# A two-layer decode kernel: the attention's matrix steps in column tiles of 32, and work moved between the engines

## The chip, the cores and the metric

The kernel runs on one core of a Trainium2 chip. The core has TensorE (PE in the profile; its weight loads are PEld), VectorE (DVE), ScalarE (ACT), GpSimd (POOL), and SyncE (SP), which here issues the transfers. 16 DMA engines carry data from the device's memory (HBM) into the on-chip memory of 128 partitions. TensorE writes into accumulator banks of 128 x 512 fp32 words. The metric is the device time of one execution in microseconds. The kernel before took 1196.09 us in the median of three runs (1195.54 to 1197.15).

## The reference, cut to what matters

One token for each of 8 batch elements goes twice through attention and a dense block; both rounds use the same caches and weights:

```python
x = x + A(layernorm(x));  x = x + B(layernorm(x))     # and the same two lines again
def A(x):                       # B=8, D=512, 32 query heads on 8 kv heads, 8192 keys of 128
    q = x @ wq                  # [8, 32, 128]
    p = softmax(q . k_cache / sqrt(128))
    return (p @ v_cache) @ wo   # caches [8, 8, 8192, 128] bf16
def B(x): return silu(x @ w1) @ w2          # 512 -> 1792 -> 512
```

Each cache holds 134 MB, far more than on-chip memory, and both are needed in both rounds.

## The kernel before, in words

*Tasks and positions.* A task is one round, batch element and kv head: 2 x 8 x 8 = 128 tasks. A task has 8 positions of 1,024 keys; two positions are a granule, the unit of a load: 2,048 keys x 128 channels of bf16, 0.524 MB. `make_tasks` mixes both rounds. For 5 of 8 kv heads (20 granules) K stays on chip between the rounds, so that it is loaded once: 352 loads of K in all, and 512 of V.

*Loads.* An arena of 27 slots (`NSLOT`) takes the granules. `plan_loads` sorts all loads by the position that needs them and gives each the slot that is free first. SP issues them in that order (`issue_until`, lines 411 to 413), each when the last reader of its slot is done. `issue` (L357) builds the source. For K, partition p receives 16 neighbouring keys, 4 KB, with a step of 64 keys (16 KB) from one partition to the next; a V granule is contiguous, 4 KB for each partition:

```python
src = cache[d.b, d.g].rearrange("(p k c) d -> k p (c d)", k=NGRAN, p=128)[d.k]   # K, L360
src = cache[d.b, d.g].rearrange("(k p c) d -> k p (c d)", k=NGRAN, p=128)[d.k]   # V, L362
```

*The steps of a task.* `emit_t` (L440): one VectorE transpose of 32x32 blocks per K granule, in place. `emit_q`: four matmuls spread the query over the rows and a VectorE multiply (L466) makes QB. `emit_s` (L473): scores, 32 matmuls per granule; four of them write to partition groups 0, 32, 64 and 96 of a bank, the form that the profile calls 128*32. Then the softmax: `softmax_max` takes the row maxima (L491) and spreads them (L493), `softmax_shift` brings them to all rows by a matmul with ones (L501) and takes the minimum of each row (L504, L507), `softmax_exp` (L511) exponentiates on ScalarE and sums each row, `softmax_sum` gathers the sums of a head (L518) and adds them over the partitions on GpSimd (L521), `emit_pt` transposes P with four matmuls (L530) and copies it to PT (L534), and `softmax_rcp` takes reciprocals (L541). `emit_pv` (L543): 64 matmuls per task with a V chunk as the stationary operand and 4 columns of PT, each repeated 12 times (`PVN`), as the moving one: 128 x 48 into OTp. `emit_norm` (L561) multiplies by the reciprocals.

*Between the attentions.* `wo_part` adds each head's product with wo in the bank MISC; `block_stages` holds residual, LayerNorm (`ln_stages`), both dense projections (`project`) and silu. For all but the last batch element of a round these are single-token pieces of a list `chain`, a few of which are put between the positions; at the very end the last round runs for all 8 tokens at once (the tail).

*Order.* One loop over positions p (L770) writes every engine's program. At odd p it emits the scores of positions p - 1 and p, and PV for positions that lie `LP` = 14 back; the softmax steps of the task before come at the phases in `soft`; the transposes run `LT` = 2 positions ahead. Each engine works strictly in the order written, and waits on semaphores that `Sync` derives from named resources.

Of the kernel before, what the change touches and what calls it, by code (L numbers as in the profile page):

```python
# [5 lines left out]
HQ = 32  # L6
DH = 128
# [5 lines left out]
GRP = 8  # L13
# [6 lines left out]
LP = 14  # L20
EARLY = 4
WO_FROM = 36
NTP = 2
# [7 lines left out]
PVN = 12  # L31
# [177 lines left out]
def _build(ctx, nc, A_x, A_k_cache, A_v_cache, A_wq, A_wo, B_w1, B_w2, out):  # L209
# [63 lines left out]
    own_q = sb([128, NQ], FP32, "own_q")  # L273
    pick = sb([128, NPART, 128], BF16, "pick")
# [5 lines left out]
    s1 = sb([128, B], FP32, "s1")  # L280
    s1a = sb([128, B], FP32, "s1a")
# [3 lines left out]
    eh = sb([128, FT * B], FP32, "eh")  # L285
# [5 lines left out]
    ones = sb([128, 128], FP32, "ones")  # L291
# [9 lines left out]
    ssa = [sb([128, REP], FP32, "ssa") for _ in range(NST)]  # L301
# [6 lines left out]
    QSp = ps_bank("QSp")  # L308

# [47 lines left out]
    def issue(d):  # L357
        cache = A_k_cache if d.kind == "K" else A_v_cache
        if d.kind == "K":
            src = cache[d.b, d.g].rearrange("(p k c) d -> k p (c d)", k=NGRAN, p=128)[d.k]  # L360
        else:
            src = cache[d.b, d.g].rearrange("(k p c) d -> k p (c d)", k=NGRAN, p=128)[d.k]  # L362
        dst = ARENA[:, d.slot * SLOT:(d.slot + 1) * SLOT]
        dma(sp, dst, src, slsem[d.slot], writes=[r_half(d.slot, 0), r_half(d.slot, 1)])
        (k_slot if d.kind == "K" else v_slot)[(d.b, d.g, d.k)] = d.slot

    with nc.Block() as block:

        @block.sync
        def _(sync_eng):  # L370
# [11 lines left out]
            op(dve, lambda: dve.memset(ones[:, :], 1.0), writes=["ones"])  # L382
            for n in range(NQB):
                op(pool, lambda n=n: pool.memset(QB[n][:, :, :], 0.0), writes=[f"QB{n}"])
# [9 lines left out]
                own_q[:, :], ident[:, :].rearrange("p (c q) -> p c q", q=QUAD), AX.X, ALU.add),  # L394
               reads=["ident"], writes=["own_q"])
            for i in range(NPART):
                op(dve, lambda i=i: dve.tensor_copy(
                    pick[:, i, :].rearrange("p (a r) -> p a r", a=NQ),
                    ident[:, i // 2 * 2 * QUAD:(i // 2 + 1) * 2 * QUAD].rearrange("p (r e) -> p e r", e=2)[:, i % 2]
                    .unsqueeze(1).to_broadcast([128, NQ, QUAD])),  # L400
                   reads=["ident"], writes=["pick"])
            for c in range(NQ):
# [4 lines left out]
                   reads=["hm", "real"], writes=["far"])  # L407

# [44 lines left out]
            def emit_q(ti):  # L453
# [7 lines left out]
                for i in range(NPART):  # L461
                    at = (n * NPART + i) * REP
                    steps.append(lambda i=i, at=at: pe.matmul(  # L463
                        QSp[:, at:at + REP], pick[:, i, :], q, start=True, stop=True))
                mm_group(steps, reads=["pick", rq], writes=[f"QS{n}"])
                op(dve, lambda: dve.tensor_tensor(  # L466
                    QB[n][:, :, 0:USED].rearrange("p i (r a) -> p i r a", a=NQ),
                    QSp[:, n * NPART * REP:(n + 1) * NPART * REP].rearrange("p (i r) -> p i r", r=REP).unsqueeze(3)
                    .to_broadcast([128, NPART, REP, NQ]),
                    own_q[:, :].unsqueeze(1).unsqueeze(1).to_broadcast([128, NPART, REP, NQ]), ALU.mult),  # L470
                   reads=[f"QS{n}", "own_q"], writes=[f"QB{n}"])
# [17 lines left out]
            def softmax_max(ti):  # L489
# [3 lines left out]
                op(dve, lambda: dve.tensor_scalar(  # L493
                    spread[:, :].rearrange("p (c q) -> p c q", q=USED), lanes, rowmax[:, 0:1], -SM_SCALE,
                    op0=ALU.mult, op1=ALU.mult),
                   reads=["ident", "rowmax"], writes=["spread"])

            def softmax_shift(ti):
                ob = ti % 2
                every = OTp[ob][:, 0:NQ * USED]  # L500
                mm_group([lambda: pe.matmul(every, ones[:, :], spread[:, :], start=True, stop=True)],  # L501
# [7 lines left out]
            def softmax_exp(ti):  # L509
                bank, st = ti % NSCP, ti % NST  # L510
                op(act, lambda: act.activation(  # L511
                    P[:, :].rearrange("p (x j k) -> p k x j", x=CPB, k=NGRAN),
                    SCp[bank][:, :].rearrange("p (k x j) -> p k x j", k=NGRAN, x=CPB), ACT.Exp, bias=shift[:, 0:1], scale=SM_SCALE, accum_out=rs[st][:, :]),
                   reads=[f"SC{bank}", "shift"], writes=["P", f"rs{st}"])

            def softmax_sum(ti):
                st = ti % NST
                op(dve, lambda: dve.tensor_scalar(  # L518
                    ssm[st][:, :], hm[:, :], rs[st][:, 0:1], None, op0=ALU.mult),
                   reads=["hm", f"rs{st}"], writes=[f"ssm{st}"])  # L520
                op(pool, lambda: pool.partition_all_reduce(ssa[st][:, :], ssm[st][:, :], 128, bass.bass_isa.ReduceOp.add),  # L521
                   reads=[f"ssm{st}"], writes=[f"ssa{st}"])

            def emit_pt(ti):
# [5 lines left out]
                    lambda c=c: pe.transpose(tpv[:, c, :], P[:, c * 128:(c + 1) * 128], ident[:, :])  # L530
                    for c in range(CPB)
                ]
                mm_group(steps, reads=["P", "ident"], writes=[f"TP{tb}"])
                op(dve, lambda: dve.tensor_copy(  # L534
# [4 lines left out]
            def softmax_rcp(ti):  # L539
                st = ti % NST  # L540
                op(dve, lambda: dve.reciprocal(rcp[st][:, :], ssa[st][:, :]), reads=[f"ssa{st}"], writes=[f"rcp{st}"])  # L541

            def emit_pv(i):  # L543
# [5 lines left out]
                otp = OTp[ob][:, 0:REP * PVN].rearrange("p (r n) -> p r n", n=PVN)  # L549
                steps = []  # L550
                for c in range(GRP):
                    cc = (i % GPT) * GRP + c
                    steps.append(
                        lambda c=c, cc=cc: pe.matmul(  # L554
                            otp, chunk(slot, h * GRP + c), pv[:, cc % CPB, cc // CPB % NQ, k, :].unsqueeze(2).to_broadcast([128, REP, PVN]),
                            start=(cc == 0), stop=(cc == NCH - 1),
                        )
                    )
                mm_group(steps, reads=[r_half(slot, h), f"PT{pb}"], writes=[f"OT{ob}"])

            def emit_norm(ti):  # L561
# [6 lines left out]
                op(dve, lambda: dve.tensor_tensor(dst, OTp[ob][:, 0:REP * PVN:PVN], rcp[st][:, :], ALU.mult),  # L568
                   reads=[f"OT{ob}", f"rcp{st}"], writes=[rd])

            def ln_stages(xv, rx, n):

                xcv, sqv, xnv = xc[:, :, 0:n], sq[:, :, 0:n], xnT[:, :, 0:n]

                def first():
                    op(dve, lambda: dve.tensor_reduce(s1[:, 0:n], xv.rearrange("p k b -> p b k"), AX.X, ALU.add),
                       reads=[rx], writes=["s1"])
                    op(pool, lambda: pool.partition_all_reduce(s1a[:, 0:n], s1[:, 0:n], 128, bass.bass_isa.ReduceOp.add),
                       reads=["s1"], writes=["s1a"])

                def second():
                    op(
                        dve,
                        lambda: dve.scalar_tensor_tensor(
                            xcv, s1a[:, 0:n].unsqueeze(1).to_broadcast([128, KT, n]), -1.0 / D, xv,
                            op0=ALU.mult, op1=ALU.add,
                        ),
                        reads=["s1a", rx], writes=["xc"],
                    )
                    op(dve, lambda: dve.tensor_tensor(sqv, xcv, xcv, ALU.mult), reads=["xc"], writes=["sq"])  # L590
                    op(dve, lambda: dve.tensor_reduce(s1[:, 0:n], sqv.rearrange("p k b -> p b k"), AX.X, ALU.add),
                       reads=["sq"], writes=["s1"])
                    op(pool, lambda: pool.partition_all_reduce(s1a[:, 0:n], s1[:, 0:n], 128, bass.bass_isa.ReduceOp.add),
# [265 lines left out]
```

## Time and profile before

| What | Value |
|---|---|
| median of three runs | 1196.09 us |
| the profiled execution's own time | 1198.79 us |
| its span, first to last instruction | 1197.1 us |
| busy: PE, PEld | 839.0 us (70%), 673.4 us (56%) |
| busy: DVE, ACT, POOL | 736.1 (61%), 183.5 (15%), 70.8 us (6%) |
| bytes moved by DMA | 468.06 MB, mean 391 GB/s |
| mean granted TensorE clock | 0.663 |

In the page's rows by slices each digit is the busy share of one fortieth of the span in tenths. In a group of instructions the line number, engine and operation come first, then output and inputs by the program's names, shapes and count, then busy time, mean duration in ns, and the engine's idle time before the group with what ended it. "Time to landing" of a load runs from its issue to the arrival of its last byte. Rows by stretches give start and end, length, busy time of PE, PEld, DVE, ACT and POOL with instruction counts, the granted clock, the mean busy share of the 16 DMA engines and the rate in GB/s.

### The profile page before, as it was taken

To read this page: it belongs to the slowest core of one execution; us is meant where nothing else is said; L and a number is where in the kernel's file an instruction comes from. 1 tells how busy PE (TensorE), PEld (TensorE's weight loads), DVE (VectorE), ACT (ScalarE), POOL (GpSimd) and SP (SyncE) were. 2 spreads that over 40 slices of the span, in tenths; PEclk is the share of its full clock that TensorE was granted. 3 is DMA by queue.
4 is the path that set the end of the run, shared out by engine and by line. 5 is a ranking of instruction groups with operands and counts; after the bars stand their busy time and mean duration, and the time that the engine had idled before them with its cause. 6 is when DMAs were issued, how large, how long until landed. Compare 5 with 4: busy or idle time off the path is not lost.

```text
span 1197.1 us, 46189 instructions
## 1 busy us (share of the span) xinstructions
PE 839.0 (70%) x20984; PEld 673.4 (56%) x20984; DVE 736.1 (61%) x1830; ACT 183.5 (15%) x266; POOL 70.8 (6%) x172
## 2 busy tenths in 40 slices
PE   1636677767776677767777778777776777677785
PEld 1435566556655566556665566556665656555564
DVE  3736763767456673867457763867376755768464
ACT  0101112111111012111111111111111111111111
POOL 0000000000000000000000000000000000000000
PEclk9955568555765577655866586756775587657765
DMA  9999999999999999999999999999999999999994
GB/s 368 385 396 397 399 355 408 407 394 395 393 408 407 368 389 401 408 404 395 389 408 408 388 397 409 407 402 395 393 407 403 399 393 408 407 392 386 402 408 165
DMA packets 131619, 468.06 MB, mean 391 GB/s; under 512 B 13904, under 2 KB 19808, under 8 KB 130912
## 3 DMA queue, kind: packets, MB, share of 16 engines
q1 hardware_dynamic: 131424, 465.12, 99.1%
q8 instruction: 164, 2.69, 0.9%
q14 instruction: 31, 0.25, 0.1%
HBM read 465.05 MB, written 0.01 MB: 388 GB/s over the span
## 4 chain that ended last, share of the span: by engine, by line
DMA 40%; PE 31%; DVE 15%; issue 9%; SPq 3%; ACT 2%; POOL 0%; POOLq 0%; ACTq 0%; DVEq 0%
DMA arena<-in_A_v_cache_dram 37%; PE OTp L554 14%; PE SCp L481 8%; DVE arena L444 7%; SPq L339 3%; DMA arena<-in_A_k_cache_dram 3%; PE MISC L634 3%; PE OTp L501 2%; PE TPp L530 2%; ACT P L511 2%; DVE rowmax L491 1%; DVE PT L534 1%; PE MISC L652 1%; DVE tr L607 1%; DVE spread L493 1%
## 5 line engine op out<-in xcount | busy, mean ns | idle before, releaser
L554 PE MATMUL OTp<-PT,arena 128*128 128x48 bf16 x8192 | 381.1, 205 | 227.6 <-DMA arena<-in_A_v_cache_dram 182.1
L444 DVE STREAM_TRANSPOSE arena<-arena 128x1024 int32<-128x1024 int32 x352 | 434.9, 1236 | 115.9 <-DMA arena<-in_A_k_cache_dram 115.2
L554 PEld LDWEIGHTS OTp<-PT,arena 128*128 128x128 bf16 x8192 | 316.9, 110 | 331.5 <-DMA arena<-in_A_v_cache_dram 242.6
L511 ACT ACTIVATE P<-SCp,shift 128x512 bf16<-128x512 f32 x128 | 180.3, 1409 | 930.6 <-DVE shift L507 651.5
L481 PE MATMUL SCp<-arena,QB 128*32 128x128 bf16 x8192 | 287.0, 275 | 37.3 <-issue 29.0
L481 PEld LDWEIGHTS SCp<-arena,QB 128*32 128x32 bf16 x8192 | 161.4, 115 | 84.1 <-issue 48.6
L521 POOL PARTITION_ALL_REDUCE ssa<-ssm x128 | 55.6, 435 | 996.0 <-DVE ssm L518 970.8
L534 DVE COPY PT<-TPp 128x256 bf16<-128x256 bf16 x128 | 37.3, 291 | 103.6 <-PE TPp L530 101.8
L501 PE MATMUL OTp<-spread,ones 128*128 128x64 f32 x256 | 75.4, 389 | 25.9 <-DVE spread L493 22.7
L491 DVE TENSOR_REDUCE rowmax<-SCp 128x1 f32<-128x512 f32 x128 | 84.8, 663 | 11.5 <-PE SCp L481 10.3
L530 PE MATMUL TPp<-ident,P 128*128 128x128 bf16 x512 | 68.8, 278 | 13.7 <-ACT P L511 9.6
L504 DVE SCALAR_TENSOR_TENSOR own<-OTp,real,far 128x64 f32<-128x64 f32 x128 | 32.9, 257 | 71.7 <-PE OTp L501 71.7
L501 PEld LDWEIGHTS OTp<-spread,ones 128*128 128x128 f32 x256 | 54.9, 266 | 35.6 <-DVE spread L493 34.4
L518 DVE TENSOR_SCALAR ssm<-hm,rs 128x4 f32<-128x4 f32 x128 | 26.8, 210 | 73.9 <-ACT P L511 73.9
L530 PEld LDWEIGHTS TPp<-ident,P 128*128 128x128 bf16 x512 | 41.7, 122 | 16.5 <-ACT P L511 12.3
L634 PE MATMUL MISC<-xnT,wq 128*128 128x32 bf16 (+1 forms) x1152 | 37.1, 185 | 19.3 <-DVE xnT L621 13.1
L634 PEld LDWEIGHTS MISC<-xnT,wq 128*128 128x128 bf16 x1152 | 35.8, 105 | 20.4 <-issue 16.3
L652 PE MATMUL MISC<-at,wo 128*128 128x32 bf16 x1024 | 37.7, 185 | 6.1 <-issue 4.4
L652 PEld LDWEIGHTS MISC<-at,wo 128*128 128x128 bf16 x1024 | 33.2, 103 | 6.9 <-issue 4.6
L463 PE MATMUL QSp<-QT,pick 128*128 128x4 bf16 x512 | 32.5, 168 | 5.7 <-DVE QT L717 2.9
L493 DVE TENSOR_SCALAR spread<-ident,rowmax 128x64 f32<-128x64 bf16 x128 | 32.6, 255 | 4.5
L511 ACT ACTIVATION_READ_ACCUMULATOR P<-SCp,shift 128x1 f32 x128 | 33.3, 260 | 0.0
(54 smaller groups left out, 276.3 us busy)
## 6 DMA issues: line engine op xcount, KB each, us to landing
arena<-in_A_v_cache_dram SPq DMA_DIRECT2D x512, 512.0 KB, 10.3
arena<-in_A_k_cache_dram SPq DMA_DIRECT2D x352, 512.0 KB, 14.5
wq<-in_A_wq_dram SPq DMA_DIRECT2D x1, 4096.0 KB, 16.6
wo<-in_A_wo_dram SPq DMA_DIRECT2D x1, 4096.0 KB, 26.3
w<-in_B_w_dram SPq DMA_DIRECT2D x2, 1792.0 KB, 22.8
P<-in_A_x_dram SPq DMA_DIRECT2D x1, 8.0 KB
out_dram<-P SPq DMA_DIRECT2D x1, 8.0 KB
```

The lines of the kernel that those rows point to most:

```text
L444: op(dve, lambda: dve.transpose(words, words), reads=[r_half(slot, 0), r_half(slot, 1)], writes=[r_half(slot, 0), r_half(slot, 1)])
L481: lambda n=n, t=t: pe.matmul(SCp[bank][t * QUAD:(t + 1) * QUAD, k * 128:(k + 1) * 128], QB[qn][:, n, :], keys[:, t, n // 2, n % 2], start= ...
L491: op(dve, lambda: dve.tensor_reduce(rowmax[:, :], SCp[bank][:, :], AX.X, ALU.max), reads=[f"SC{bank}"], writes=["rowmax"])
L493: op(dve, lambda: dve.tensor_scalar(spread[:, :].rearrange("p (c q) -> p c q", q=USED), lanes, rowmax[:, 0:1], -SM_SCALE, op0=ALU.mult, op ...
L501: mm_group([lambda: pe.matmul(every, ones[:, :], spread[:, :], start=True, stop=True)], reads=["ones", "spread"], writes=[f"OT{ob}"])
L511: op(act, lambda: act.activation(P[:, :].rearrange("p (x j k) -> p k x j", x=CPB, k=NGRAN), SCp[bank][:, :].rearrange("p (k x j) -> p k x ...
L521: op(pool, lambda: pool.partition_all_reduce(ssa[st][:, :], ssm[st][:, :], 128, bass.bass_isa.ReduceOp.add), reads=[f"ssm{st}"], writes=[f ...
L530: lambda c=c: pe.transpose(tpv[:, c, :], P[:, c * 128:(c + 1) * 128], ident[:, :])
L534: op(dve, lambda: dve.tensor_copy(PT[pb][:, :, :].rearrange("p x (c q) -> p x c q", q=USED), tpv.rearrange("p x (c q) -> p x c q", q=QUAD) ...
L554: lambda c=c, cc=cc: pe.matmul(otp, chunk(slot, h * GRP + c), pv[:, cc % CPB, cc // CPB % NQ, k, :].unsqueeze(2).to_broadcast([128, REP, P ...
L634: lambda o=o, k=k: pe.matmul(MISC[:, o * n:o * n + w], w_sb[:, k, o * 128:(o + 1) * 128], rhs_of(k).to_broadcast([128, w]) if n == 1 else ...
L652: lambda o=o, h=h: pe.matmul(MISC[:, o * w:(o + 1) * w], wo_sb[:, h, o * 128:(o + 1) * 128], rhs_of(h).to_broadcast([128, w]) if n == 1 el ...
```

## The change

The keys of a K granule are dealt to the partitions differently: partition 32a + j takes 16 keys from block a (2,048 keys) of the head, so the source is 4 blocks of 32 neighbouring pieces of 4 KB. A granule's P can then be transposed in pieces of 32 columns, and `softmax_exp` writes P without reordering. All attention matmuls write to groups of 32 partitions: query spreading (16 matmuls per task), the spreading of the maxima (4), transposes (16), and PV, which now has 4 columns of PT as the stationary operand and a V chunk of 128 columns as the moving one, in four partition groups whose partial sums `emit_fold` adds. Sums over partitions (softmax and LayerNorm) become matmuls with ones, residuals matmuls with the identity. ScalarE takes the copies out of the accumulator banks and the two scalings (spread, ssm); GpSimd takes the Newton steps of the single-token LayerNorm and the products of silu, which is computed from tanh instead of exp. `LP` goes from 14 to 12, and the phases of the softmax steps change (`SOFT`). The diff, cut to its core:

```diff
-LP = 14
+LP = 12
+SOFT = (0, 1, 2, 3, 4, 4, 6)
-NTP = 2
+NTP = 1
-PVN = 12
...
         if d.kind == "K":
-            src = cache[d.b, d.g].rearrange("(p k c) d -> k p (c d)", k=NGRAN, p=128)[d.k]
+            src = cache[d.b, d.g].rearrange("(a k j c) d -> k a j (c d)", a=NQ, k=NGRAN, j=QUAD)[d.k]
...
-                    steps.append(lambda i=i, at=at: pe.matmul(
-                        QSp[:, at:at + REP], pick[:, i, :], q, start=True, stop=True))
...
+                    for a in range(NQ):
+                        steps.append(lambda a=a, at=at, pairs=pairs: pe.matmul(
+                            QSp[a * QUAD:(a + 1) * QUAD, at + a:at + USED:NQ], pairs, q, start=True, stop=True))
+                mm_group(steps, reads=["ident", rq], writes=["QS"])
+                op(act, lambda: act.copy(
+                    QB[n][:, :, 0:USED],
...
-                op(dve, lambda: dve.tensor_scalar(
-                    spread[:, :].rearrange("p (c q) -> p c q", q=USED), lanes, rowmax[:, 0:1], -SM_SCALE,
+                op(act, lambda: act.activation(
+                    spread[:, :].rearrange("p (c q) -> p c q", q=USED), lanes, ACT.Copy, scale=rowmax[:, 0:1]),
...
-                mm_group([lambda: pe.matmul(every, ones[:, :], spread[:, :], start=True, stop=True)],
+                mm_group([lambda t=t: pe.matmul(every[t * QUAD:(t + 1) * QUAD, :], ones[:, :], spread[:, :], start=True, stop=True)
+                          for t in range(NQ)],
...
-                    P[:, :].rearrange("p (x j k) -> p k x j", x=CPB, k=NGRAN),
-                    SCp[bank][:, :].rearrange("p (k x j) -> p k x j", k=NGRAN, x=CPB), ACT.Exp, bias=shift[:, 0:1], scale=SM_SCALE, accum_out=rs[st][:, :]),
+                    P[:, :], SCp[bank][:, :], ACT.Exp, bias=shift[:, 0:1], scale=SM_SCALE, accum_out=rs[st][:, :]),
...
+                op(act, lambda: act.activation(ssm[st][:, :], hm[:, :], ACT.Copy, scale=rs[st][:, 0:1]),
...
-                op(pool, lambda: pool.partition_all_reduce(ssa[st][:, :], ssm[st][:, :], 128, bass.bass_isa.ReduceOp.add),
-                   reads=[f"ssm{st}"], writes=[f"ssa{st}"])
+            def softmax_all(ti):
+                st = ti % NST
+                mm_group([lambda t=t: pe.matmul(sums[t * QUAD:(t + 1) * QUAD, :], ones[:, :], ssm[st][:, :],
+                                                start=True, stop=True) for t in range(NQ)],
...
+                        tpv[k * QUAD:(k + 1) * QUAD, c, :], P[:, k * 128 + c * QUAD:k * 128 + (c + 1) * QUAD], ident[:, :])
+                    for c in range(CPB) for k in range(NGRAN)
...
-                op(dve, lambda: dve.tensor_copy(
+                op(act, lambda: act.copy(
                     PT[pb][:, :, :].rearrange("p x (c q) -> p x c q", q=USED),
...
-                            otp, chunk(slot, h * GRP + c), pv[:, cc % CPB, cc // CPB % NQ, k, :].unsqueeze(2).to_broadcast([128, REP, PVN]),
-                            start=(cc == 0), stop=(cc == NCH - 1),
+                            OTp[ob][t * QUAD:t * QUAD + REP, 0:DH], pv[:, cc % CPB, cc // CPB % NQ, k, :], chunk(slot, h * GRP + c),
+                            start=(cc < NQ), stop=(cc >= NCH - NQ),
...
+            def emit_fold(ti):
+                ob = ti % 2
+                op(act, lambda: act.copy(OS[:, :], OTp[ob][:, 0:DH]), reads=[f"OT{ob}"], writes=["OS"])
+                folded = OTp[ob][:, DH + NQ * USED:DH + NQ * USED + REP]
+                mm_group([lambda t=t: pe.matmul(folded[t * QUAD:(t + 1) * QUAD, :], OS[:, t * QUAD:(t + 1) * QUAD], pick[:, :],
...
+                    mm_group(steps, reads=[rx, "ident", "mean"], writes=["MISC"])
+                    op(act, lambda: act.activation(sqv, mid, ACT.Square), reads=["MISC"], writes=["sq"])
+                    op(act, lambda: act.copy(xcv, mid), reads=["MISC"], writes=["xc"])
...
-                            op(dve, lambda: dve.tensor_scalar(t, y, y, v, op0=ALU.mult, op1=ALU.mult),
+                            op(pool, lambda: pool.tensor_scalar(t, y, y, v, op0=ALU.mult, op1=ALU.mult),
...
+                    op(act, lambda: act.activation(th[:, 0:FT * n], MISC[:, 0:FT * n], ACT.Tanh, scale=0.5),
+                       reads=["MISC"], writes=["th"])
...
+                    op(pool, lambda: pool.tensor_scalar(th[:, 0:FT * n], th[:, 0:FT * n], 1.0, None, op0=ALU.add),
+                       reads=["th"], writes=["th"])
+                    op(pool, lambda: pool.tensor_tensor(hsT[:, 0:FT * n], th[:, 0:FT * n], hx[:, 0:FT * n], ALU.mult),
+                       reads=["th", "hx"], writes=["hsT"])
...
-            soft = {0: [softmax_max], 2: [softmax_shift, softmax_exp], 4: [softmax_sum], 5: [emit_pt], 7: [softmax_rcp]}
+            stages = (softmax_max, softmax_shift, softmax_exp, softmax_sum, emit_pt, softmax_all, softmax_rcp)
+            soft = {ph: [f for f, at in zip(stages, SOFT) if at == ph] for ph in SOFT}
...
+                    emit_fold(tj)
                     emit_norm(tj)
```

## The prediction

> **What bounds the kernel now.** I read the header and the slices first, then the DMA queues, then the chain that ended last, and then the DMA share and the landing times stage by stage. The page:
>
> ```profile
> span 1197.1 us, 46189 instructions
> PE   1636677767776677767777778777776777677785
> DMA  9999999999999999999999999999999999999994
> GB/s 368 385 396 397 399 355 408 407 394 395 393 408 407 368 389 401 408 404 395 389 408 408 388 397 409 407 402 395 393 407 403 399 393 408 407 392 386 402 408 165
> q1 hardware_dynamic: 131424, 465.12, 99.1%
> DMA 40%; PE 31%; DVE 15%; issue 9%; SPq 3%; ACT 2%; POOL 0%; POOLq 0%; ACTq 0%; DVEq 0%
> DMA arena<-in_A_v_cache_dram 37%; PE OTp L554 14%; PE SCp L481 8%; DVE arena L444 7%; SPq L339 3%; DMA arena<-in_A_k_cache_dram 3%; PE MISC L634 3%; PE OTp L501 2%; PE TPp L530 2%; ACT P L511 2%; DVE rowmax L491 1%; DVE PT L534 1%; PE MISC L652 1%; DVE tr L607 1%; DVE spread L493 1%
> ```
>
> The 16 DMA engines are busy in every slice, while PE rests a quarter of most of them; the chain's largest member is the wait for V. So the bound is the transport of 465 MB. The stretches (start:end, length, busy of PE, PEld, DVE, ACT, POOL, clock, DMA share, GB/s):
>
> ```profile
> 200.00:260.00 60.00, 41.13 (x931) 31.73 (x931) 37.89 (x81) 9.03 (x14) 3.02 (x7) 0.57 1.03 407
> 260.00:320.00 60.00, 44.98 (x1150) 37.14 (x1143) 41.15 (x109) 8.64 (x13) 4.21 (x10) 0.60 1.00 386
> 320.00:345.00 25.00, 18.82 (x514) 14.99 (x514) 7.56 (x31) 5.66 (x8) 1.72 (x4) 0.80 1.03 409
> 10.00:15.00 5.00, 0.24 (x4) 0.18 (x4) 2.53 (x13) 0.00 (x0) 0.59 (x3) 1.00 1.02 431
> 1181.00:1182.00 1.00, 0.71 (x19) 0.58 (x16) 0.00 (x0) 0.00 (x0) 0.00 (x0) 0.50 0.03 12
> ```
>
> When fed, the engines together move 407 to 409 GB/s, 25.5 GB/s each. In 260 to 320 us, where 20 of the 27 slots hold kept K and 7 are left for the stream, it is 386. The last data lands at 1182 us. How full the queue is, is seen in the time from issue to landing, first from 220 to 260 us, then from 265 to 315 us:
>
> ```profile
> arena<-in_A_k_cache_dram SPq DMA_DIRECT2D x11, 512.0 KB, 15.8
> ...
> arena<-in_A_k_cache_dram SPq DMA_DIRECT2D x14, 512.0 KB, 7.2
> ```
>
> A load of 0.524 MB takes 1.28 us at 408 GB/s, so some 12 loads are in flight in the first and 5 to 6 in the second. Last, groups that the change touches (busy, mean ns):
>
> ```profile
> L554 PE MATMUL OTp<-PT,arena 128*128 128x48 bf16 x8192 | 381.1, 205 | 227.6 <-DMA arena<-in_A_v_cache_dram 182.1
> L481 PE MATMUL SCp<-arena,QB 128*32 128x128 bf16 x8192 | 287.0, 275 | 37.3 <-issue 29.0
> L511 ACT ACTIVATE P<-SCp,shift 128x512 bf16<-128x512 f32 x128 | 180.3, 1409 | 930.6 <-DVE shift L507 651.5
> L534 DVE COPY PT<-TPp 128x256 bf16<-128x256 bf16 x128 | 37.3, 291 | 103.6 <-PE TPp L530 101.8
> L493 DVE TENSOR_SCALAR spread<-ident,rowmax 128x64 f32<-128x64 bf16 x128 | 32.6, 255 | 4.5
> L521 POOL PARTITION_ALL_REDUCE ssa<-ssm x128 | 55.6, 435 | 996.0 <-DVE ssm L518 970.8
> ```
>
> **The change, part by part.**
>
> *VectorE to ScalarE.* Four VectorE steps per task leave: spread 0.255, ssm 0.210, PT 0.291, QB 0.218 us, together 0.97 us, times 128 = 125 us of its 736. ScalarE takes them and one more, the copy of 128x128 sums per task; by its nearest rows (0.18 us for 14 elements, 0.27 for 112, 1.41 for 512 strided) that is 1.1 to 1.9 us per task, 140 to 240 us on top of 184. ScalarE is idle 85% of the span, VectorE 39%. Cover: the DMA stream, 9.35 us per task. Without that cover it would be on the path from the scores to P, see the third rival.
>
> *TensorE.* PV's 8,192 matmuls of 48 columns become 128 columns in four column tiles, the form that scores already have (8,192, four abreast): 0.35 instead of 0.47 ms, that is 287 us by the scores' row instead of 381: 94 us less. Added per task: 12 transposes, 12 query matmuls, 3 spread, 4 sums, 4 folds, 35 small ones; at the 0.17 to 0.28 us of the rows if each ran alone 6 to 10 us per task, four abreast 1.5 to 2.5 us, 190 to 320 us in all; so PE may end between 100 us less and 230 us more than 839. At zero to the end, while the stream takes longer; the first rival pays for it otherwise.
>
> *GpSimd.* 128 all-reduces of 0.435 us go, with 36 of LayerNorm (14 us); 7 small steps per LayerNorm of one row come, 16 times, and 2 per silu. Off the path: they sit in the chain that has most of a batch element (some 130 us) to finish. In the tail (n = 8) the Newton steps stay on VectorE; two all-reduces of 0.41 us, a residual and a reciprocal of 0.85 us go, copies of some 0.25 us and matmuls come: 15.1 us from the last data to the end, plus or minus 2.
>
> *Order.* LP falls from 14 to 12 and P's transposes come one position earlier; the slots are as many, and each K and V is loaded as often. Bytes are unchanged: 352 K loads and 512 V loads of 0.524 MB, 12.06 MB of weights.
>
> *The K load.* Before, the source is 128 rows of 4 KB at a constant step of 16 KB; after, it is 4 blocks of 32 rows, block step 512 KB, row step 4 KB. 128 partitions at one step still receive it. No row of before shows how such a load is shared out, since all 864 loads there count 128 rows in one step on both sides. Two ends: all 16 engines go on sharing it (then it costs nothing, and gains nothing, since the stretches with K run at 407 as those with nearly V alone at 409), or it is cut along the outermost count, which is now 4 on one side and 128 on the other, so only four shares can be made, 32 rows each. I take the second: one count per side is all that a cut into equal shares can use here, as the source can't be written with 128 at one step, and equal shares of 128 rows and of 4 blocks are four at most. If the same four engines take them each time:
> K 352 x 131,072 B = 46.14 MB on each of the four; V 512 x 32,768 B = 16.78; weights 0.75; instructions (2.9 MB over 16) 0.18; in all 63.85 MB instead of 29.3.
> At 25.5 GB/s (408 over 16) that is 2,504 us. Before the stream 4.5 us, after it 15: span 2,523, and the profiled execution had 1.7 us outside its span (1198.79, 2.7 over the median of 1196.09), so 2,525 us.
> The bounds of the rate: 431 GB/s was the best 5 us (26.9 each, 2,391 us), 386 the starved stretch (24.1 each, 2,668 us). I take 25.5, the rate wherever the queue was full, since here it always is: a K load lasts 5.1 us on its four engines, a pair of K and V 6.4 us, and the work of a pair is one transpose of 1.24 us and two PE groups of 0.6 to 0.8 each.
> [...]
>
> What is late next: V's shares on the four engines queue behind K's, so transposes of K and PV both wait; SP stands in front of a full queue, and all other engines idle. None of the gains above can show.
>
> **Rivals.**
> 1. *K stays on all 16 engines (faster).* For: the present loads do, at a share of 1.03; against: the pattern above. Then the stream stays the bound: 468 MB at 408 is 1,147 us, with 21 around it 1,168, if the shorter PE and VectorE work lets slots free earlier in the 7-slot stretches; with their dips left, about 1,196. I give 1,180. It decides at 16 shares; at 8 the same sum gives 23.07 + 16.78 + 0.93 = 40.8 MB, 1,599 us and another 21, slower already.
> 2. *Four engines, and they starve.* In the stretches with 7 slots (24 pairs per batch element, 192 in all) a slot comes free only after its load's work; with 3 us of that bare per pair, 580 us more: 3,100. For: the 386 GB/s there now. Against: 7 slots hold 22 us of work at 3.2 us a load, the waiting K and the work in hand take some 13.
> 3. *Sixteen engines, and the softmax chain shows (slower, little).* From row maxima to the transposes: spread 0.25, spread matmuls 0.7, own 0.26, shift 0.22, Exp 1.41 and 0.26, handoffs 0.5 = 3.6 us, against one pair of loads, 2.57 us, since the transposes come a pair earlier. 1.0 us x 128 = 130 us at most; half of it bare: 1,250. Against: TensorE has 30% to spare and slots absorb it.
> (That the four engines differ from load to load, so that all 16 are filled, gives rival 1's time.)
>
> **How the numbers follow.** Four engines, fed: 0.83, predicted 2,525, own range 2,380 to 2,700 (the two rates above, with a little for starvation). Rival 1: 0.09, of which 0.02 with no difference. Rival 2: 0.04. Rival 3: 0.04. 0.2% is about what a measurement of this kernel can tell (three runs spread by 0.13%). Faster 0.07, same 0.02, slower 0.91. The range is the first case's, which leaves some 2 in 10 out.
>
> **What would show it.** Right: the mean DMA share falls to about 0.45 (29.3 MB of mean load over 63.85), mean rate near 185 GB/s, K's time to landing well over 15 us, the chain of waits mostly DMA with K's part large, PE, DVE and ACT idle on DMA, and stretches with K slow while those with V alone are not. Of the rest: DVE busy near 590 us, ACT 310 to 400, POOL below 30, PV's group near 290 us (clock aside). Wrong: a share near 1 and 400 GB/s, and then the dips between 260 and 320 us decide between 1,168 and 1,196.

## The result and the profile after

The changed kernel takes 2,755.7 us in the median of four runs (2,744.6 to 2,776.4), the kernel before 1,196.6 us in four: a ratio of 2.304, 95% interval 2.290 to 2.318. The forecast had the direction and nearly all of the size (2,525 us), but the time lies 56 us above the end of its range. The profiled execution is the slowest of the four, 2,776.4 us with a span of 2,774.6 us; the steps below are weighed against it.

From the page of the changed kernel: header, slices of PE, DMA and rate, DMA queues, chain that ended last, and two groups (busy us, mean ns, then the idle time before the group and what ended it).

```profile
span 2774.6 us, 60270 instructions
PE   1111234122331135222342235222431234122243
DMA  4554446444554447444564447444644456444564
GB/s 149 175 180 142 153 153 238 150 144 148 173 209 148 150 147 243 157 145 142 183 209 151 154 152 243 154 153 152 232 163 151 149 160 237 146 154 148 166 232 126
q1 hardware_dynamic: 127200, 465.10, 50.5%
q8 instruction: 218, 3.57, 0.5%
DMA 53%; SPq 35%; PE 6%; issue 3%; ACT 1%; DVE 1%; POOLq 0%; POOL 0%; ACTq 0%; DVEq 0%
L445 DVE STREAM_TRANSPOSE arena<-arena 128x1024 int32<-128x1024 int32 x352 | 438.0, 1245 | 1795.2 <-DMA arena<-in_A_k_cache_dram 1795.2
L562 PE MATMUL OTp<-arena,PT 128*4 128x128 bf16 x8192 | 308.1, 295 | 1776.3 <-DMA arena<-in_A_v_cache_dram 1753.6
```

The same 465 MB flow, but the DMA engines are busy half of the time, in a slice as in the mean, and the rate sits near 150 GB/s. VectorE waits 1,795 us for K, TensorE 1,754 us for V, and the chain is DMA and SP in front of a full queue (88% together: SP 35%, the landing of V 49%, of K 4%). Six slices of 232 to 243 GB/s hold more V. Four stretches of 1 us show the cycle (start:end, length, busy of PE, PEld, DVE, ACT, POOL, clock, DMA share, GB/s):

```profile
572.00:573.00 1.00, 0.00 (x0) 0.00 (x0) 0.00 (x0) 0.00 (x0) 0.00 (x0) 0.50 0.27 111
574.00:575.00 1.00, 0.00 (x0) 0.00 (x0) 1.00 (x1) 0.00 (x0) 0.00 (x0) 0.50 1.01 274
575.00:576.00 1.00, 0.03 (x4) 0.03 (x8) 0.20 (x2) 0.00 (x0) 0.00 (x0) 0.50 0.97 217
579.00:580.00 1.00, 0.00 (x0) 0.00 (x0) 0.00 (x0) 0.00 (x0) 0.00 (x0) 0.50 0.25 102
```

A share of a quarter is four engines of sixteen: they carry K alone, at 102 to 111 GB/s (a K load by itself shows the same share and 105 GB/s further down). Between such pieces all sixteen are busy, and move only 217 to 274 GB/s. That second fact was not in the forecast.

### The profile page after: what moved, and what is told of

Read it like the earlier page. It is cut to its first block, busy times and chain, and to the rows that moved or that the text cites. A ratio compares the mean times of both kernels' runs of the same rounds, so it can differ in the third digit from the quotient of the medians.

```text
span 2774.6 us, 60270 instructions
## 1 busy us (share of the span) xinstructions
PE 799.3 (29%) x27880; PEld 622.3 (22%) x27880; DVE 614.3 (22%) x1081; ACT 289.3 (10%) x978; POOL 39.3 (1%) x138
## 4 chain that ended last, share of the span: by engine, by line
DMA 53%; SPq 35%; PE 6%; issue 3%; ACT 1%; DVE 1%; POOLq 0%; POOL 0%; ACTq 0%; DVEq 0%
DMA arena<-in_A_v_cache_dram 49%; SPq L339 35%; DMA arena<-in_A_k_cache_dram 4%; PE OTp L562 3%; PE SCp L486 2%; ACT P L516 1%; PE TPp L537 1%; PE OTp L505 0%; ACT PT L542 0%; PE OTp L573 0%; DVE arena L445 0%; ACT OS L571 0%; PE MISC L673 0%; SPq L91 0%; DVE own L509 0%
## 5 line engine op out<-in xcount | busy, mean ns | idle before, releaser
L562 PE MATMUL OTp<-arena,PT 128*4 128x128 bf16 x8192 | 308.1, 295 | 1776.3 <-DMA arena<-in_A_v_cache_dram 1753.6
L562 PEld LDWEIGHTS OTp<-arena,PT 128*4 128x4 bf16 x8192 | 175.3, 107 | 1875.5 <-DMA arena<-in_A_v_cache_dram 1848.4
L486 PEld LDWEIGHTS SCp<-arena,QB 128*32 128x32 bf16 x8192 | 214.0, 132 | 30.3 <-issue 24.6
L498 ACT ACTIVATE spread<-ident,rowmax 128x64 f32<-128x64 bf16 x128 | 44.5, 347 | 1489.7 <-DVE rowmax L496 1489.7
L516 ACT ACTIVATE P<-SCp,shift 128x512 bf16<-128x512 f32 x128 | 88.0, 688 | 175.0 <-DVE shift L512 136.2
L542 ACT COPY PT<-TPp 128x256 bf16<-128x256 bf16 x128 | 47.7, 373 | 516.1 <-PE SMp L527 446.8
L537 PE MATMUL TPp<-ident,P 128*32 128x128 bf16 x2048 | 79.0, 296 | 34.8 <-ACT P L516 28.5
L537 PEld LDWEIGHTS TPp<-ident,P 128*32 128x32 bf16 x2048 | 53.7, 134 | 45.2 <-ACT P L516 37.9
L505 PE MATMUL OTp<-spread,ones 128*32 128x64 f32 x1024 | 55.5, 304 | 21.3 <-ACT spread L498 14.3
L522 ACT ACTIVATE ssm<-hm,rs 128x4 f32<-128x4 f32 x128 | 38.1, 297 | 3.6
```

The costliest lines, as they stand in the source:

```text
L486: lambda n=n, t=t: pe.matmul(SCp[bank][t * QUAD:(t + 1) * QUAD, k * 128:(k + 1) * 128], QB[qn][:, n, :], keys[:, t, n // 2, n % 2], start= ...
L498: op(act, lambda: act.activation(spread[:, :].rearrange("p (c q) -> p c q", q=USED), lanes, ACT.Copy, scale=rowmax[:, 0:1]), reads=["ident ...
L505: mm_group([lambda t=t: pe.matmul(every[t * QUAD:(t + 1) * QUAD, :], ones[:, :], spread[:, :], start=True, stop=True) for t in range(NQ)], ...
L516: op(act, lambda: act.activation(P[:, :], SCp[bank][:, :], ACT.Exp, bias=shift[:, 0:1], scale=SM_SCALE, accum_out=rs[st][:, :]), reads=[f" ...
L537: lambda c=c, k=k: pe.transpose(tpv[k * QUAD:(k + 1) * QUAD, c, :], P[:, k * 128 + c * QUAD:k * 128 + (c + 1) * QUAD], ident[:, :])
L542: op(act, lambda: act.copy(PT[pb][:, :, :].rearrange("p x (c q) -> p x c q", q=USED), tpv.rearrange("p x (c q) -> p x c q", q=QUAD)[:, :, ...
```

## The experiments

### Is it the K source, and does the number of engines follow its outermost count?

The change as a whole mixes many edits, so the kernel before got only the new form of the K source, with 4, 8 and 16 blocks. A fourth kernel is the changed one with each K granule fetched by four loads of 32 neighbouring rows.

```diff
 # e2, e3, e4 on the kernel before, N = 4, 8, 16
-src = cache[d.b, d.g].rearrange("(p k c) d -> k p (c d)", k=NGRAN, p=128)[d.k]
+src = cache[d.b, d.g].rearrange("(a k j c) d -> k a j (c d)", a=N, k=NGRAN, j=128 // N)[d.k]
 # e1 on the changed kernel, for K
-dma(sp, dst, src, slsem[d.slot], ...)
+for t in range(NQ):
+    sp.dma_start(dst[t * QUAD:(t + 1) * QUAD, :], src[t]).then_inc(slsem[d.slot].sem, 16)
```

> The kernel after, with each K granule brought by four loads of 32 partitions (source 32 rows of 4 KB) instead of one load with a source of 4 blocks x 32 rows; the bytes, slots and order stay. Theory (the one K load is cut in four shares, and four of the 16 engines carry all of K): all 16 engines carry K again, 468 MB at 408 GB/s plus 21 us around it: 1,168 to 1,200 us, DMA share near 1. Rival (the longer ScalarE chain and the TensorE waits make the time): stays above 2,000 us. Rival (the change of order by itself costs a little): 1,220 to 1,330.

> The kernel before with the K load's source alone taken from the change (4 blocks x 32 rows); the rows of K then meet other rows of V, so the sums mix wrong keys, at the same amount of work. Theory: this alone makes the slowdown: 63.85 MB on each of four engines, 2,525 us at 25.5 GB/s each, 2,755 at the rate that the changed kernel shows. Rival (other parts of the change cost the most): below 1,500.

> The kernel before with the K source as 8 blocks x 16 rows (again other keys, same work). Theory (the outermost count gives the number of engines): 8 engines carry K, 40.8 MB each: 1,620 us at 25.5 GB/s, 1,770 at the rate of the changed kernel. Rival (any source of two steps is slow, whatever its count): near 2,525 to 2,755. Rival (only the count 4 is a special case): 1,196.

> The kernel before with the K source as 16 blocks x 8 rows (other keys, same work). Theory: 16 engines as before, 1,185 to 1,205 us. Rival (a source of two steps is slow by itself): well above 1,300.

Measured: 2,739.8 us with 4 blocks, 2,092.3 with 8 and 1,787.0 with 16, each in one execution, and 1,855.6 in the median of four for the four loads (ratio to the kernel before 1.549, 1.543 to 1.555). The DMA queue's rows, in the order 4, 8, 16 blocks and four loads:

```profile
q1 hardware_dynamic: 127200, 465.10, 51.2%
```

```profile
q1 hardware_dynamic: 128608, 465.10, 75.9%
```

```profile
q1 hardware_dynamic: 131424, 465.12, 100.6%
```

```profile
q1 hardware_dynamic: 148320, 465.18, 99.6%
```

The run with 4 blocks settles where the time comes from: one edited line makes the kernel before as slow as the changed one. The shares of 51, 76 and 101% say that more engines are busy as the blocks grow from 4 to 16. Both kernels that keep all engines busy were expected near 1,200 us, and are 590 and 660 us off. A stretch of the one with 16 blocks (columns as above):

```profile
300.00:320.00 20.00, 8.00 (x174) 6.36 (x174) 7.09 (x14) 1.41 (x2) 0.43 (x1) 0.50 1.03 250
```

The share is 1.03, as in the kernel before at 407 GB/s, and the rate is 250. A busy engine is not an engine at its rate: by these two rows (16 engines times the share, over the rate) a row of 4 KB occupies an engine for 0.27 us here and for 0.17 us there.

### The loads alone: what sets the rate of an engine

The next kernels compute nothing and only load, stage after stage, so that nothing can starve the queue.

```
rows of 4 KB into an arena of 27 slots; blocks(n, each): n blocks of `each` neighbouring rows
e6:  128 rows at one step (4, 16, 36 KB); blocks 16x8, 8x16, 4x32 with a far and a near step; pairs of 4x32 and V
e7:  32 rows into the quarters in turn; 32 rows into partitions 0-31; 64 into 0-63; 8x4, 16x4, 4x4 into parts
e11: pairs of a contiguous V load of 128 rows and a K load, blocked or at a step of 16 KB;
     two 4x32; 2x32 into 0-63 with 64 rows into 0-63, or into 64-127
e12: 2x32 into 0-63, into 32-95, and each in turn with V
e16: 4x32 and V in turn: one and one, two and two, four and four, eight and eight
```

> No computation: only loads into the 27 slots, in ten stages one after the other, each stage waited out; the output is a copy of x. Stages: 64 granules of 128 rows at one step of 4, 16 and 36 KB; 64 as 16 blocks x 8 rows with a block step of 128 KB and then 36 KB; 64 as 8 x 16 with 256 KB and 68 KB; 32 as 4 x 32 with 512 KB and 132 KB; last 32 pairs of a 4 x 32 load and a contiguous one. Theory W (a load of several blocks gives each DMA engine neighbouring partitions, and engines that write near partitions at once are in each other's way; the source's step does not matter): about 400 GB/s in the first three stages, then 170, 170, 133, 133, 91, 91, each pair of equal stages within 5%. Theory R (the step in HBM is what slows): stages 5, 7 and 9, with the odd steps, come back to 400, 204 and 102 GB/s (25.5 for each engine). Theory S (slots that come free late starve the loads): without computation all block stages run at 25.5 GB/s for each engine, 400, 204 and 102; the last stage then takes 206 us, and 225 by the other two.

> No computation, as before it, eight stages: 256 loads of 32 contiguous rows into the four quarters of the partitions in turn; 128 into partitions 0-31 only; 128 loads of 64 rows into partitions 0-63; 128 loads of 8 blocks x 4 rows into partitions 0-31, and the same into partitions 0, 2, 4 .. 62; 128 of 16 x 4 rows into 0-63; 128 of 4 x 4 rows into 0-15, and the same into 0, 8 .. 120. [...] Rival (it is the number of rows in a load, or the two steps in the source, not the place of the partitions): stages 4 and 5 alike.

Stretches of the first of these kernels (GpSimd's busy time, clock, DMA share, GB/s): 128 contiguous rows, 16 blocks of 8, 8 of 16, 4 of 32, and pairs of 4x32 and a contiguous load.

```profile
40.00:60.00 20.00, 0.00 (x0) 1.00 1.03 410
320.00:340.00 20.00, 0.00 (x0) 1.00 1.03 241
640.00:660.00 20.00, 0.00 (x0) 1.00 0.51 210
960.00:980.00 20.00, 0.00 (x0) 1.00 0.26 105
1240.00:1260.00 20.00, 0.00 (x0) 1.00 0.47 153
```

Shares of 0.26, 0.51 and 1.03 are 4, 8 and 16 engines: the cut follows the outermost count exactly. Four engines move 105 GB/s, 8 move 210, 26.2 each, but 16 move 241, 15 each. A near block step (36 KB where it was 128 KB) gives 239, so the distance in memory is not the reason. Of the three theories, S (each engine keeps its rate) holds for 4 and 8 engines and fails for 16, where W had 170. The K load of before, 128 rows at a step of 16 KB, goes at 358 to 385 GB/s by itself, and in turn with V (e11) at 410. Of the second kernel, 32 rows to the quarters in turn, 32 rows into partitions 0-31, 64 rows into 0-63, then 8 blocks of 4 rows into partitions 0-31 and into 0, 2 to 62:

```profile
40.00:60.00 20.00, 0.00 (x0) 1.00 1.04 229
180.00:200.00 20.00, 0.00 (x0) 1.00 1.05 205
280.00:300.00 20.00, 0.00 (x0) 1.00 1.03 207
420.00:440.00 20.00, 0.00 (x0) 1.00 0.49 177
520.00:540.00 20.00, 0.00 (x0) 1.00 0.51 208
```

In the first three all engines are busy again, and partitions 0-63 take no more than 0-31: 207 and 205 GB/s, what eight engines move above (210). In the last two the source is the same and only the destination differs, and the rates do too, where the rival had them alike: 0-31 gives 174 to 183 GB/s, and 0, 2 to 62 gives 195 to 208. So the destination has a part in the rate. How large it is these runs do not show: loads of 32 or 64 rows might be slow for their size as well, and no run spreads so few rows over all partitions. Which engine wrote to which partitions was not seen, so Theory W's reason is not shown, and why 16 blocks move only 241 GB/s is open.

> No computation: pairs of loads in seven stages, each waited out; the output is a copy of x. 48 pairs each of a contiguous load of 128 rows with a K load of 4 x 32, 8 x 16, 16 x 8 blocks, and of 128 rows at a step of 16 KB; 24 pairs of two loads of 4 x 32; 48 pairs of 2 x 32 rows into partitions 0-63 with a load of 64 rows, first into partitions 0-63 too, then into 64-127. The sums of the parts measured alone: 6.3, 3.8, 3.45 and 2.7 us per pair, 10.0 for two block loads, and 5.6 for each of the last two stages (36 rows on the engine that has most). Theory W (engines that write into the same half of the partitions are in each other's way): 6.9, about 5, about 4.3 and 2.6 us per pair, 10.0, then more than 6 with both loads in one half, and 5.6 with the loads in different halves. Rival (an engine loses time whenever it goes from one kind of load to the other): the last two stages alike, and both above 5.6; two block loads still 10.0.

A stage's length over its number of pairs gives the time of a pair. A pair of 4x32 and V takes 7.0 us, one of 8x16 and V 5.24 (2.50 and 1.28 alone), one of 16x8 and V 3.77, and two 4x32 in turn 10.1 (9.96 from the parts). With 2x32 rows into partitions 0-63, a load of 64 rows into 0-63 makes the pair 6.5 us and one into 64-127 6.0, where the parts were put at 5.6 for both: Theory W has the first right and the rival that both lose, neither has both. 352 pairs at 7.0 us, 160 V loads alone at 1.3 and 12 MB of weights at 408 GB/s are 2,464 + 208 + 30 = 2,702 us, with 21 us of start and tail 2,723: the kernel with 4 blocks (2,740) without any of its computation. With 5.24 the sum is 2,103 (8 blocks: 2,092). With 3.77 it is 1,586, 200 us short of 16 blocks; that one is not explained by pairs. Nor are the four loads of 32 rows: with K at the 229 GB/s above, 2.29 us, and V at 1.28 the same sum gives 1,515, 340 short of 1,856.

What makes a pair of 6.26 us (4.98 and 1.28) last 7.0?

> Loads alone, nothing computed (the output is a copy of x). Four stages of 48 loads or pairs: two blocks of 32 K rows into partitions 0-63; two blocks of 32 into 32-95; pairs of the first with a contiguous 128-row load into all partitions; pairs of the second with the same contiguous load. What is asked: why a 4x32 load with a contiguous load behind it costs 6.9 to 7.0 us where the two alone cost 6.3. [...] Theory B: any load of few engines loses when one of all engines lies between; both pair stages are alike, within 0.1 us. [...]

> Loads alone, nothing computed (the output is a copy of x). Four stages of 48 K loads (4 blocks of 32 rows) and 48 contiguous V loads each: one K and one V in turn; two and two; four and four; eight and eight. What is asked: in the stage of pairs the K part goes on at its full 106 GB/s, while the V part takes about 2.0 us in place of the 1.28 us that such a load takes in a row of its kind, with the DMA engines counted as fully busy at 150 to 340 GB/s. Theory A: the loss comes where a burst of V begins, when all engines set off together; then it is paid once per burst, and a pair takes 7.0, 6.65, 6.45 and 6.35 us in the four stages. Theory B: every V load between K loads is slow, however many follow each other; then a pair takes 6.9 to 7.0 us in all four. Without any loss it would be 6.26 us in all.

With two engines (a share of 0.13, 53 GB/s) the K loads alone take 5.07 us a load at either place, and the pairs 6.69 us (partitions 0-63) and 6.79 (32-95) against 6.35 for the parts: alike, as Theory B had it, so the place of the two blocks is not what makes the loss. In bunches of one, two, four and eight, a pair takes 7.0, 6.7, 7.4 and 7.2 us, which is neither row of the expectation: not a price per burst, since bunching does not lower it, and not constant either. Stretches of that kernel, first of the pairs in turn (K, V, K), then of eight and eight (K, V):

```profile
105.00:109.00 4.00, 0.00 (x0) 1.00 0.26 105
109.00:112.00 3.00, 0.00 (x0) 1.00 0.71 214
112.00:116.00 4.00, 0.00 (x0) 1.00 0.25 100
...
1100.00:1105.00 5.00, 0.00 (x0) 1.00 0.26 106
1114.00:1127.00 13.00, 0.00 (x0) 1.00 1.01 248
```

K goes at its full 100 to 106 GB/s. The contiguous loads, 410 GB/s in their own stage, move 248 for 13 us with all engines busy. So the loss lies in V's part of the cycle, and in the way the engines work there, not in idle engines. Why V's rows take longer after blocked ones is open; in the changed kernel the rate does come back to between 402 and 420 GB/s from 444 to 456 us, where SP has issued 19 V loads in a row.

### The rest of the change, without the new K source

> The kernel after with K loaded as before (128 rows at one step of 16 KB); so that P's transposes still meet V's rows, Exp reorders P while it writes, as before (1.41 us instead of 0.69 for each of 128). All else of the change stays. Theory (the source of the K load is all of the slowdown, the rest of the change is hidden by the stream or gains a little): 1,168 to 1,200 us. Rival (the shorter chain from row maxima to PV, with LP of 12 and the copies on ScalarE, is not hidden): 1,220 to 1,330.

> The kernel after with K loaded as before (and Exp reordering P), and the order of before as well: LP 14 and the softmax steps at the old phases. Theory (the 130 us that remain with the old K load come from LP of 12 and the earlier phases, TensorE waiting for Exp and VectorE for TensorE): 1,185 to 1,230 us. Rival (they come from the steps themselves: PV's partial sums fetched by ScalarE and folded, more matmuls and hand-offs per task): 1,290 to 1,340.

> The kernel after with only the source of the K load as before, Exp writing P in order (0.69 us); the rows of K then meet other rows of V, so the sums mix wrong keys, at the same amount of work. This is the change without its K load. Theory (the chain from row maxima to PV counts): 0.7 us less per task than with the reordering Exp, 128 x 0.7 = 90 us less at most: 1,235 to 1,300. Rival (Exp's length is hidden): 1,315 to 1,340. Rival (the rest of the change gains): below 1,190.

> The kernel before with only the order of the change: LP 12, softmax steps at phases 0, 1, 2, 3, 4 and 6. Theory (the order costs): 1,230 to 1,300. Rival (the order is hidden in the old form, the steps cost): 1,190 to 1,205.

```diff
 # e9: the changed kernel with the K source of before. e5: the same, and Exp reorders P as before (P's transposes follow)
-P[:, :], SCp[bank][:, :], ACT.Exp, ...
+P[:, :].rearrange("p (x j k) -> p k x j", ...), SCp[bank][:, :].rearrange(...), ACT.Exp, ...
 # e8: e5 with the order of before
-LP = 12;  SOFT = (0, 1, 2, 3, 4, 4, 6)
+LP = 14;  SOFT = (0, 2, 2, 4, 5, 5, 7)
 # e10: the kernel before with LP = 12 and softmax phases 0, 1, 2, 3, 4, 6
```

Measured: e5 1,328.0 us (1.110, 1.108 to 1.113), e8 1,306.0 (1.092, 1.090 to 1.094), e9 1,318.8 (1.104, 1.101 to 1.107), e10 1,206.0 (1.010, 1.007 to 1.014). So the rest of the change costs 10% by itself. The order is 1 to 2% of it (11 us in the old form, 22 between e5 and e8), and halving Exp (0.69 us for 1.40) gains 9 us, which speaks against Exp as the cause. The wait lists of TensorE say where it went (waiting, waited for, us in total, times, longest us), first the kernel before, then e9:

```profile
PE OTp L554 <- DMA arena<-in_A_v_cache_dram: 182.1, 198, 16.6
PE OTp L554 <- issue: 34.6, 25, 2.8
PE SCp L481 <- issue: 29.0, 25, 2.5
```

```profile
PE OTp L562 <- issue: 94.3, 45, 4.3
PE OTp L562 <- DMA arena<-in_A_v_cache_dram: 85.9, 61, 21.6
PE SCp L486 <- issue: 84.9, 48, 4.5
```

Over all lines TensorE rests on "issue", on nothing that the profile shows, for 78.9 us in the kernel before and 292.1 in e9, while it waits less for data. Its waits for ScalarE grow as well, from 10 to 138 us, and those for VectorE fall from 67 to 4. One rest of e9, in its timeline of TensorE (start, us, what it does, and in brackets the idle time before it):

```profile
270.15 0.67 PE L486 MATMUL SCp<-arena,QB 128*32 128x128 bf16 x16
273.98 0.60 PE L562 MATMUL OTp<-arena,PT 128*4 128x128 bf16 x16 [3.16 <-issue]
```

The rests recur after about 128 pairs of weight load and matmul, or a multiple of that. The instruction queue (q8) carried 164 packets of 16 KB before and 218 with the change, 54 more; the change adds 6,896 pairs, 13,792 instructions, which is 53.9 times 256, and the 20,984 pairs of before are 163.9 times 256 instructions. So a packet holds 256 instructions of TensorE, and TensorE rests at the end of many of them. Most of the added pairs are tiny. Three kernels test whether their number is what costs.

```diff
 # e13, on the kernel before, ahead of each scores granule (the result is overwritten)
+12 x pe.matmul(SCp[bank][t * QUAD:(t + 1) * QUAD, k * 128:k * 128 + 4], ident[:, 0:QUAD], ident[:, 0:4], ...)
 # e14, likewise
+2 x pe.matmul(SCp[bank][:, k * 128:(k + 1) * 128], ident[:, :], ident[:, :], ...)
 # e15, on e9: spread, sums, fold and LayerNorm sums in one matmul each
-ones = sb([128, QUAD], FP32, "ones")
+ones = sb([128, 128], FP32, "ones")
-mm_group([lambda t=t: pe.matmul(every[t * QUAD:(t + 1) * QUAD, :], ones[:, :], spread[:, :], ...) for t in range(NQ)], ...)
+mm_group([lambda: pe.matmul(every, ones[:, :], spread[:, :], start=True, stop=True)], ...)
```

> The kernel before with 12 matmuls of four columns on a 32-column tile ahead of each scores granule (their result is overwritten). 48 more pairs of weight load and matmul in each task, 6,144 in all, which is about 48 more packets of instructions of 16 KB; their own busy time is small (about 0.2 us a granule, beside a TensorE that is busy for 839 of 1,197 us). Theory: TensorE stops for 2 to 3 us where a packet of instructions ends, and the stops are what the changed kernel loses when its K load is as before; then this one takes 1,230 to 1,310 us, the packets go from 164 to about 212, and the idle time of TensorE that waits for nothing shown goes from 79 to over 180 us. Rival: the number of instructions does not matter and the loss is the softmax chain; then at most 1,215 us.

> The kernel before with two matmuls of 128x128 ahead of each scores granule (their result is overwritten): about as much added TensorE work as the twelve tiny ones, with 8 added pairs in each task in place of 48. Theory of the instruction packets: 1,195 to 1,215 us, about 172 packets. Rival (TensorE's work or its order is what costs): the same time as with the twelve tiny matmuls.

> The changed kernel with the K source as before and P not reordered (its keys are mixed wrongly against the V rows, as in the run of 1,319 us), and with a ones tile 128 wide, so that the spread of the shift, the row sums, the fold and the LayerNorm sums are one matmul in place of four: 18 of the 46 pairs that the change adds to each task are gone, the engines and the order stay. Theory of the instruction packets: 40 to 50 us less than 1,319, so 1,265 to 1,290 us. Rival (the chain over ScalarE and TensorE): 1,310 to 1,325 us.

| Kernel | instruction packets | TensorE on "issue", us (times) | TensorE busy, us | median, us | ratio |
|---|---|---|---|---|---|
| before | 164 | 78.9 (62) | 839 | 1,196 | |
| e14, two matmuls | 172 | 93.6 (79) | 887 | 1,201.2 | 1.004 to 1.009 |
| e15, fewer matmuls | 197 | 138.4 (117) | 924 | 1,256.9 | 1.049 to 1.055 |
| e13, twelve tiny ones | 212 | 207.0 (137) | 909 | 1,287.6 | 1.074 to 1.080 |
| e9, the rest of the change | 218 | 292.1 (158) | 772 | 1,318.8 | 1.101 to 1.107 |

Time goes with the number of packets and not with TensorE's busy time: e14 adds 48 us of work and 5 us of time (0.6 us for each added packet), e13 adds 70 us of work in six times as many instructions and 91 us of time, 1.9 us for each added packet. At that price, which is an estimate for another kernel, the 54 packets of the change are 103 of its 124 us; the order adds 11. e15 gained 62 us, more than the 40 to 50 expected; its waits on ScalarE (Exp, spread and sums' copy) fell too, from 130 to 68 us, so not all of that is packets, and how much of the 124 us the waits on ScalarE make is not shown. The stops reach the end because the slots wait for TensorE: where K is kept and 7 slots are left, the stream runs dry. In e9 (columns as in the first stretches), against 377 GB/s of the kernel before in the same 20 us:

```profile
260.00:280.00 20.00, 13.33 (x512) 11.05 (x516) 14.56 (x23) 5.44 (x19) 0.00 (x0) 0.59 0.84 282
```

A stop lasts 1.3 us in the kernel before (78.9 us in 62) and 1.8 in e9 (292.1 in 158). The longest stops, 3.2 us (477.5 in 151), are in the changed kernel with four loads of 32 rows, while the changed kernel itself shows only 36 stops of 1.6 us for the same 218 packets: where TensorE waits for V anyway (1,754 us), a stop does not show. What sets a stop's length is open: the load queue's share is 99.1% at 1.3 us (the kernel before) and 99.6% at 3.2 us.

## Why the prediction came out as it did

*The cut into four shares* was right: shares of a quarter, a half and the whole (0.26, 0.51 and 1.03) for 4, 8 and 16 blocks. Which engines they are no run shows.

*63.85 MB per engine at 25.5 GB/s, 2,504 us: the step that failed, by size.* The bytes hold; the one rate for all of them does not. The forecast's pair of K and V, 6.4 us, takes 7.0 with the loads alone: over 352 pairs that is some 200 of the 231 us by which the median missed. An estimate of where in the pair: with K's 46.14 MB at 26.5 GB/s (106 over 4) they take 1,741 us, where the sum had 1,809. V and the rest, 17.71 MB on the same four engines, had 695 us and get what is left of the profiled span, 2,775 - 20 - 1,741 = 1,014 us, or 17.5 GB/s. 319 us more and 68 less are the 251 us by which the profiled execution missed. The bounds of the rate, 24.1 and 26.9, came from rows in which all loads were 128 rows at one step, so neither end could hold a loss that only a mixture shows. The argument "the rate wherever the queue was full" was the mistake: the queue was full. Why V loses its rate behind K stays open.

*Rival 2, starvation* falls: the sum from loads without computation gives 2,723 of the 2,740 us with 4 blocks.

*Rival 1, all 16 engines,* did not occur, and its threshold was wrong: "it decides at 16 shares" took the number of engines for the rate. 16 shares gave 1,787 us, and 8 gave 2,092 where its sum had 1,620. None of the variants beats the kernel before.

*Rival 3, sixteen engines and the softmax chain,* has the direction of what the rest costs with K loaded as before, and less than half of its size (54 us, with 130 at most; 124 to 133 measured), for a reason that the runs bear at most in part: a shorter Exp gains 9 us. Added instructions of TensorE are the larger part by the price above, and no step of the prediction priced an instruction beyond its duration.

*"At zero to the end" for TensorE and ScalarE* holds only under the slow stream, which was the cover named. Without that cover the rest of the change costs 124 us. Two slips in the working change nothing in the sum: "0.35 instead of 0.47 ms" should be 35 and 47 ns for each matmul by the rows it names, and "100 us less" leaves out the added matmuls (with them its terms give 96 to 226 us more; TensorE's busy time fell by 40).

*What would show it.* DMA share about 0.45, measured 0.505; near 185 GB/s, 169; DVE near 590 us, 614; ACT 310 to 400, 289, since Exp without reordering takes 0.69 us for 1.41, which the forecast did not count; POOL below 30, 39; PV's group near 290 us, 308; PE between 100 less and 230 more than 839, 799. Stretches with K are slow and those with V alone are not, as said. K's part is large in VectorE's waits (1,795 us) but only 4% of the chain, and the trace of the changed kernel gives no time to landing for K.

## What to carry to other kernels

A load's rate depends on the order in which its rows are named (410 GB/s for 128 rows at one step of 4 KB, 241 for 16 blocks of 8), and a busy share near 1 does not prove it (1.03 in both): look at share and GB/s together, and try the new load alone and between the others before a layout is built on it. Count TensorE's instructions as well as their time: where the stream is close to the bound, 256 more short ones cost 1.9 us here, beyond what their duration says. When a source must be cut in blocks, sum it with a rate measured on that mixture, not with the best rate of plain loads.

## What the runs showed of the hardware that was not expected

- Sixteen busy engines move 410 GB/s with 128 rows at one step of 4 KB, 241 with 16 blocks of 8 rows, and 205 in loads of 32 rows into partitions 0-31.
- Contiguous loads between blocked ones fall to about 250 GB/s with all engines busy, and bunching eight of them does not bring the rate back. The cause is open.
- TensorE stops 1.3 to 3.2 us at many of the ends of packets of 256 of its instructions; what sets the length is open.
